# One load of v per head pair, a value factor per pair, and the rescaling of kT moved from ScalarE to VectorE, in a clustered-attention and feed-forward kernel

## The chip, the cores and the metric

The kernel runs on one NeuronCore of a Trainium2 chip. The metric is the device time of one launch in microseconds, the median of several runs. A core has five engines with a queue of instructions each: TensorE (PE, matrix products), VectorE (DVE), ScalarE (ACT), GpSimd (POOL) and SyncE (SP), which here issues every DMA.

## The reference

```python
def _attn_ref(q, k, v, centroids):                 # B, H, S, D = 4, 8, 768, 64; 16 centroids per head
    q_n = q / (np.linalg.norm(q, axis=-1, keepdims=True) + 1e-06)   # k_n, c_n likewise
    q_assign = np.argmax(np.einsum('bhsd,hcd->bhsc', q_n, c_n), axis=-1)   # k_assign likewise
    mask = q_assign[:, :, :, None] == k_assign[:, :, None, :]
    scores = np.where(mask, D ** -0.5 * np.matmul(q, k.transpose(0, 1, 3, 2)), -1000000000.0)
    attn = np.exp(scores - np.max(scores, axis=-1, keepdims=True))
    attn = attn / (np.sum(attn, axis=-1, keepdims=True) + 1e-09)
    return np.matmul(attn, v)
x = attn_out.transpose(0, 2, 1, 3).reshape(3072, 512)
def _moe_ref(x, w_in, w_out):                      # 512 x 2048 and 2048 x 512
    h = x @ w_in
    g = np.where(h >= 1, h, np.where(h <= -1, 0.0, (h + 1) ** 2 / 4.0))
    return g @ w_out
```

## The kernel before

All products run on TensorE in 16-bit floats: a number is split into a high and a low half, and three of the four cross products are added. The work is cut into 4 batches; a batch has 4 pairs of heads (`hp`) and 3 chunks of 256 queries; batch and chunk together are the 12 units `u` of the feed-forward part.

For each batch and pair, `kv_load` brings k, q and v (384 KB each) into the pair's slot (`kvq`). `kv_scale` squares k and q on ACT and makes a scale per tensor from the sum (tiles `sc`, `phi`, `es`). `kq_split` and `v_split` (both through `split`) write high and low halves, ACT the high ones, DVE the low ones; `transpose` turns k and q by DMA. `assign` multiplies kT and qT with the centroids, finds the cluster of each token by five DVE steps on `mx` and `z1`, writes a one-hot row into the natural tiles `kn` and `qn` (tiles `n`, for the first batch also `x`, `g`, `o`), scales k's second half by `phi` on POOL (`n<-n,phi`) and kT by `phi` on ACT (`kvq<-kvq,phi`), writes q's high half a second time on ACT (`n<-kvq,sc`), and transposes both again (`k1`, `q1`). The scale of v is one per batch: `v_bound` takes the largest |v| of a pair on DVE (`v_am`), for batches 1 to 3 from a load of v of its own, 384 KB per pair into the tile `x` or `o`, ahead of the batch; `batch_scale` makes `sv` and `isx` from the four.

`at_scores` multiplies a query tile with all keys into PSUM (`bank`), with DVE reducing it (`sS`, `sbi`); `at_soft` takes the exponential on ACT, splits it (`hl`: ACT the cast, POOL the difference), and transposes it by DMA into `pT`, or early in the program by PE; `at_av` multiplies by the values, spreads 1/sum over PSUM, copies that on ACT (`rb<-banka`), multiplies on DVE and splits the result into `x`. `ffn1` and `ffn2` are the two products with the weights, with `r` and `g` between them: DVE, ACT, DVE, ACT cast, POOL difference.

The weights come in 16 pieces (512 KB; here each float arrives as two 32-bit words). `w_load` brings a piece to a staging place that the table `RAW` names (three places of `w`, the last two pieces in halves through `wk`); `w_bits` and `w_split` turn it into two halves with four ACT passes of 128x1024 per piece (two named `w<-w` or `wk<-w`, one `w<-w,w_sw`, one CAST), two DVE passes and two POOL passes.

The order within each engine comes from a planner in the kernel (`Recorder`, L38 to L292): every operation is recorded with a step from a table at the end of the function, and `forward` and `backward` lay them out by the prices of `price` in eight rounds. All rows of the trace therefore bear the line L292.

Of the kernel before, what the change touches and what calls it, by code (L numbers as in the profile page):

```python
# [37 lines left out]
class Recorder:  # L38
# [37 lines left out]
    def price(self, eng, op, out, ins, kw):  # L76
# [274 lines left out]
def tile_clustered_attention_moe(  # L351
# [38 lines left out]
    RAW = [0, 1, 2, 0, 1, 2, 0, 1, 0, 2, 0, 1, 0, 0, None, None]  # L390
# [20 lines left out]
    rings["vb"] = rings["o"]  # L411
# [14 lines left out]
    hid = Ring([bank_h] + halves)  # L426
    spare = Ring([x[:, 384:] for x in halves])
# [5 lines left out]
    def misc(*shape):  # L433
        return (row_banks if early() else hid)(*shape, dtype=F32)
# [26 lines left out]
    tab = const.tile([P, 1], F32, name="tab")  # L461
    rec.scalar.activation(out=tab, in_=ones[:, :1], func=AF.Sqrt)

    def centroids():
# [5 lines left out]
        nrm = const.tile([P, 1], F32, name="c_nrm")  # L470
# [3 lines left out]
        rn = const.tile([P, 1], F32, name="c_rn")  # L474
# [16 lines left out]
    def v_bound(b, hp):  # L491

        if b == 0:
            st = view(slots[hp][:, 2304:3072], [2 * T * D], F32)
        else:
            st = view(rings["x"].bufs[2], [2 * T * D], F32) if b == 1 else new("vb", [2 * T * D], F32)
            rec.sync.dma_start(st.rearrange("p (h f) -> p h f", h=2), heads(v, b, hp))
        e = BX.setdefault(b, {})
        if hp == 0:
            e["am"] = new("v_am", [NP], BF16, 2)  # L500
        rec.vector.tensor_reduce(
            out=e["am"][:, hp : hp + 1], in_=st, op=ALU.max, axis=AX.X, apply_absolute_value=True
        )

    def to_scale(iv, sc):

        tiny_and(iv, iv, EXP_MASK)
        rec.vector.tensor_scalar(out=iv, in0=iv, scalar1=TINY, scalar2=2.0**-11, op0=ALU.max, op1=ALU.mult)  # L510
        rec.vector.reciprocal(sc, iv)

    def batch_scale(b):

        e = BX[b]
        ar = misc(NP + 1)
        rec.tensor.matmul(ar[:, :NP], ones, e["am"], start=True, stop=True)
        mx = ar[:, NP:]
        isx, sv = new("isx", [1], F32, 3), new("sv", [1], F32, 3)
        rec.vector.tensor_reduce(out=mx, in_=ar[:, :NP], op=ALU.max, axis=AX.X)  # L520
        to_scale(mx, sv)
        rec.vector.tensor_copy(isx, mx)
        e.update(isx=isx, sv=sv)
# [13 lines left out]
    def kv_scale(b, hp):  # L537
        e = KV[b, hp]
        am = new("am", [2], F32, 2)
        for i, x in enumerate("kq"):  # L540
# [20 lines left out]
        rec.vector.reciprocal(sc, iv)  # L561
# [3 lines left out]
        raw, ri = ar[:, 2:3], ar[:, 3:4]  # L565
# [13 lines left out]
    def transpose(out, nat):  # L579
        rec.sync.dma_start_transpose(out=out, in_=nat.rearrange("p n a d -> p (n a d)"))  # L580

    def kq_split(b, hp):

        e = KV[b, hp]
        for x, lower, at in (("k", 0, 0), ("q", 1, 4)):
# [5 lines left out]
            transpose(e[x + "T"], nat)  # L591
# [518 lines left out]
```

## Time and profile before

| | |
|---|---|
| median of 3 runs | 921.69 us (919.97 to 922.86) |
| the profiled execution | 923.2 us, of which the trace spans 921.4 us |
| busy in the span: PE, ACT, DVE, POOL | 812.9, 691.6, 604.1, 565.6 us |
| DMA: moved, mean rate | 144.39 MB, 157 GB/s |
| HBM: read, written | 40.40 MB, 6.29 MB |

The span has a start, up to some 145 us, in which weights and the first batch are prepared and PE is idle for more than half of the time, and a long remainder in which PE is busy nearly throughout. A row of a window table shows which of the two a stretch is. The rows come from the one profiled execution, the median from runs without a profile.

### The profile page before, as it was taken

The page shows a single profiled execution, that of the slowest core. Times are in us where ns is not written, and L with a number is a line of the kernel's source. Part 1 is how long each engine was busy: PE and PEld are TensorE (multiplying, and loading weights), DVE is VectorE, ACT ScalarE, POOL GpSimd, SP SyncE. Part 2 cuts the span into 40 slices and gives each one's busy share as a digit, 9 for nine tenths or more (in the row PEclk, how much of TensorE's full clock was granted, in tenths as well). Part 3 has the DMA queues.
Part 4 walks back from the last instruction along what each step waited for, and adds up shares of the span by engine and source line. Part 5 has one row for each costly group of instructions (what it writes and reads, how often), then busy time and mean ns, then how long its engine had stood idle before and what let it go on. Part 6 is the DMA issues. An engine that isn't in the chain of part 4 may idle for free.

```text
span 921.4 us, 19471 instructions
## 1 busy us (share of the span) xinstructions
PE 812.9 (88%) x7414; PEld 559.2 (61%) x7414; DVE 604.1 (66%) x1322; ACT 691.6 (75%) x1173; POOL 565.6 (61%) x520
## 2 busy tenths in 40 slices
PE   0256668988998999999989999998998999999998
PEld 0234446655766766676666666766666666666664
DVE  5998777887888565646776665547886555554222
ACT  6989997977778677778868778777887677777232
POOL 1766786975565577765555667655656677666221
PEclk9998789999999999999999999999999999999999
DMA  9979956796899958978999778888899768576100
GB/s 293 251 176 218 238 127 145 155 188 139 200 179 159 189 109 144 181 130 193 196 186 163 147 150 166 149 175 170 184 179 174 136 136 129 108 130 113 19 24 24
DMA packets 409535, 144.39 MB, mean 157 GB/s; under 512 B 386272, under 2 KB 401632, under 8 KB 409440
## 3 DMA queue, kind: packets, MB, share of 16 engines
q1 hardware_dynamic: 409440, 143.14, 77.0%
q8 instruction: 58, 0.95, 0.4%
q14 instruction: 37, 0.30, 0.1%
HBM read 40.40 MB, written 6.29 MB: 51 GB/s over the span
## 4 chain that ended last, share of the span: by engine, by line
PE 65%; DVE 10%; ACT 6%; issue 5%; POOL 3%; ACTq 0%; DVEq 0%; POOLq 0%
PE bank L292 47%; PE banka L292 10%; PE bankh L292 8%; DVE sS L292 3%; DVE r L292 2%; ACT sS L292 2%; DVE bank L292 2%; POOL hl L292 1%; ACT w L292 1%; DVE bankh L292 1%; DVE mx L292 1%; ACT hl L292 1%; POOL g L292 1%; ACT r L292 1%; DVE n L292 0%
## 5 line engine op out<-in xcount | busy, mean ns | idle before, releaser
L292 POOL TENSOR_TENSOR hl<-sS,hl 128x768 f16<-128x768 f32 x181 | 303.9, 1683 | 148.7 <-ACT hl L292 115.9
L292 PE MATMUL bank<-w,g 128*128 128x512 f16 x1152 | 271.1, 379 | 0.3 <-POOL g L292 0.2
L292 PEld LDWEIGHTS <-w 128*128 128x128 f16 x2304 | 224.4, 98 | 66.8 <-issue 23.0
L292 DVE CUSTOM_DVE_ANT_0 sS<-bank,zero,er 128x768 f32<-128x768 f32 x192 | 194.3, 1012 | 97.7 <-PE bank L292 67.8
L292 PEld LDWEIGHTS <-kvq 128*64 128x64 f16 (+1 forms) x3264 | 191.1, 106 | 86.2 <-issue 41.3
L292 ACT ACTIVATE sS<-sS,sbi 128x768 f32<-128x768 f32 x192 | 179.2, 933 | 83.9 <-DVE sbi L292 80.2
L292 POOL TENSOR_TENSOR g<-r,g 128x512 f16<-128x512 f32 x96 | 112.6, 1173 | 122.8 <-ACT g L292 119.2
L292 PEld LDWEIGHTS <-g 128*128 128x128 f16 x1152 | 110.7, 98 | 119.1 <-issue 2.1
L292 PE MATMUL bank<-kvq 128*128 128x384 f16 x768 | 162.4, 336 | 19.3 <-DVE sbi L292 14.1
L292 ACT CAST hl<-sS 128x768 f16<-128x768 f32 x181 | 148.3, 825 | 4.9 <-DMA pT<-hl 3.7
L292 PE MATMUL bank<-x,w 128*128 128x256 f16 x1032 | 123.9, 272 | 10.5 <-DVE r L292 5.2
L292 ACT ACTIVATE r<-r,f_ra,f_rs 128x512 f32<-128x512 f32 x96 | 77.8, 810 | 70.7 <-DVE r L292 69.7
L292 PE MATMUL banka<-pT,kvq 128*64 128x256 f16 x1728 | 106.4, 279 | 0.0
L292 DVE TENSOR_SCALAR r<-bank,f_lo,f_hi 128x512 f32<-128x512 f32 x64 | 51.6, 807 | 51.0 <-PE bank L292 41.9
L292 POOL TENSOR_TENSOR w<-w 128x1024 f32<-128x1024 f32 (+1 forms) x28 | 59.8, 2143 | 33.9 <-ACT w L292 32.0
L292 ACT CAST g<-r 128x512 f16<-128x512 f32 x96 | 58.8, 612 | 25.2 <-DVE r L292 18.7
L292 DVE SCALAR_TENSOR_TENSOR r<-bank,f_gs,r 128x512 f32<-128x512 f32 x64 | 47.9, 749 | 24.3 <-ACT r L292 15.6
L292 PE MATMUL bank<-wk,w 128*128 128x256 f16 x504 | 61.1, 272 | 3.1 <-DVE bank L292 2.1
L292 PE MATMUL bankh<-x,w 128*128 128x256 f16 x504 | 60.1, 273 | 2.2 <-DVE r L292 2.0
L292 PEld LDWEIGHTS <-ones 128*128 128x128 bf16 x244 | 17.2, 107 | 53.5 <-issue 38.5
L292 DVE TENSOR_SCALAR r<-bankh,f_lo,f_hi 128x512 f32<-128x512 f32 x32 | 25.8, 806 | 25.4 <-PE bankh L292 19.8
L292 ACT ACTIVATE n<-kvq,sc 128x768 f16<-128x768 f32 x42 | 37.1, 924 | 1.7 <-DVE sc L292 1.6
(158 smaller groups left out, 842.5 us busy)
## 6 DMA issues: line engine op xcount, KB each, us to landing
w<-in_moe_w_in_dram SPq DMA_DIRECT2D x14, 512.0 KB, 4.8
w<-in_moe_w_out_dram SPq DMA_DIRECT2D x14, 512.0 KB, 4.7
kvq<-in_k_dram SPq DMA_DIRECT2D x16, 384.0 KB, 3.6
kvq<-in_q_dram SPq DMA_DIRECT2D x16, 384.0 KB, 3.8
kvq<-in_v_dram SPq DMA_DIRECT2D x16, 384.0 KB, 4.1
out_dram<-o SPq DMA_DIRECT2D x11, 512.0 KB, 3.0
o<-in_v_dram SPq DMA_DIRECT2D x8, 384.0 KB, 3.7
pT<-hl SPq DMA_TRANSPOSE x181, 4.0
```

The lines of the kernel that those rows point to most:

```text
L292: fn(*args, **kw)
```

## The change

- `v_bound` is gone, with its own loads of v (12 of 384 KB). `kv_scale` takes the pair's |v| maximum from the slot, on DVE, and makes a value scale per pair (third column of `sc`) with three small DVE steps; `v_split` uses it. `batch_scale` forms the batch's common scale `isx` and a factor per pair, `conv`, which ACT multiplies in when it copies 1/sum (`rb<-banka,conv`).
- In `assign`, kT is scaled by `phi` on DVE instead of ACT. The halves of k and q change places, so that q's high half needs no second writing, and POOL's scaling of k stands ahead of the one-hot.
- The four transposes of the very first pair are made by PE, with eight copies from PSUM, four on ACT and four on DVE.
- Weights are staged in eight places; 15 pieces come whole, one in halves. In the last unit `r` is taken from the three buffers of `hl` instead of one.
- The planner's price of TensorE work changes, and with it the whole order.

```diff
-            if op == "transpose":
-                n *= 2
-            elif ins[1].dtype == F32:
+            if ins[1].dtype == F32:
                 n *= 4
-            return n / 4.8 + 1.2 if half else max(n / 2.4 + 2.5, 24)
+
+            return n / 4.8 + 9 if half else max(n / 2.4 + 2.5, 24)
...
-    RAW = [0, 1, 2, 0, 1, 2, 0, 1, 0, 2, 0, 1, 0, 0, None, None]
+    RAW = [3, 4, 5, 6, 7, 4, 5, 6, 0, 7, 6, 7, 0, 7, 0, None]
...
-    rings["vb"] = rings["o"]
...
-    def v_bound(b, hp):
...
-            st = view(rings["x"].bufs[2], [2 * T * D], F32) if b == 1 else new("vb", [2 * T * D], F32)
-            rec.sync.dma_start(st.rearrange("p (h f) -> p h f", h=2), heads(v, b, hp))
...
+        isx, sv, conv = new("isx", [1], F32, 3), new("sv", [1], F32), new("conv", [NP], F32, 2)
+        rec.vector.tensor_reduce(out=isx, in_=e["iv"], op=ALU.max, axis=AX.X)
+        rec.vector.reciprocal(sv, isx)
+        rec.vector.tensor_scalar(out=conv, in0=e["iv"], scalar1=sv, scalar2=None, op0=ALU.mult)
...
+        rec.vector.tensor_reduce(
+            out=am[:, 2:], in_=e["v"].rearrange("p j f -> p (j f)"), op=ALU.max, axis=AX.X, apply_absolute_value=True
+        )
...
+        tiny_and(mv, mv, EXP_MASK)
+        rec.vector.tensor_scalar(out=iv, in0=mv, scalar1=TINY, scalar2=2.0**-11, op0=ALU.max, op1=ALU.mult)
+        rec.vector.reciprocal(sc[:, 2:], iv)
...
-    def transpose(out, nat):
-        rec.sync.dma_start_transpose(out=out, in_=nat.rearrange("p n a d -> p (n a d)"))
+    def transpose(b, hp, out, nat):
+        nat = nat.rearrange("p n a d -> p (n a d)")
+        if b or hp >= 1:
+            rec.sync.dma_start_transpose(out=out, in_=nat)
+            return
...
+                    rec.tensor.transpose(ps[:, x, i * P : (i + 1) * P], nat[:, (x * T + i) * P : (x * T + i + 1) * P], idb)
+            eng = (rec.scalar.copy, rec.vector.tensor_copy)[x]
+            eng(out[:, x], ps[:, x, : T * P])
...
-        for x, lower, at in (("k", 0, 0), ("q", 1, 4)):
+        for x, lower, at in (("k", 1, 0), ("q", 0, 4)):
...
-        split(vs[:, 0], vs[:, 1], e["v"], BX[b]["sv"])
+        split(vs[:, 0], vs[:, 1], e["v"], e["sc"][:, 2:])
...
+            out=kn[:, :, 1], in0=kn[:, :, 0], in1=e["phi"].unsqueeze(2).to_broadcast([P, n2, D]), op=ALU.mult
...
-        rec.scalar.activation(out=kf, in_=kf, func=AF.Copy, scale=e["phi"])
-        qf = e["q"].rearrange("p j (t d) -> p (j t) d", d=D)
-        rec.scalar.activation(out=qn[:, :, 1], in_=qf, func=AF.Copy, scale=e["sc"][:, 1:2])
...
+        rec.vector.tensor_scalar(out=kf, in0=kf, scalar1=e["phi"], scalar2=None, op0=ALU.mult)
...
-        rec.scalar.copy(rs, rb)
+        rec.scalar.activation(out=rs, in_=rb, func=AF.Copy, scale=BX[b]["conv"][:, hp : hp + 1])
...
-        r = new("r", [2 * CQ], F32, 1)
+
+        r = new("hl" if u == NU - 1 else "r", [2 * CQ], F32, 1)
...
-            at((b - 1) * SB + 22 + hp * 3 if b else PRO + 1, v_bound, b, hp)
-        at(b * SB - 13 if b else -7, batch_scale, b)
+        at(b * SB + LA - 0.6, batch_scale, b)
...
-        t0 = PRO + 2 + i if last is None else wat[last] + 0.1
+        t0 = max(PRO + 2 + i, -1 if not RAW[i] else PRO) if last is None else wat[last] + 0.1
```

What the order of the engines becomes, at three places. ACT in the start, where the first pair (slot `kvq_61`) has been assigned; `x_69` and `x_70` are the natural tiles of the third pair, `w_76` or `w_73` the weights. Before:

```order
L292 ACTIVATE x_70,am_135<-kvq_63 128x768
L292 ACTIVATE w_76<-w_76,w_sw_157 128x1024
L292 ACTIVATE wk_66<-w_76 128x1024
L292 CAST w_76<-w_76 128x1024
L292 ACTIVATE n_73<-kvq_61,sc_137 128x12x64
L292 ACTIVATE kvq_61<-kvq_61,phi_141 128x1536
```

After:

```order
L291 ACTIVATE g_71,am_127<-kvq_64 128x768
L291 ACTIVATE wk_66<-w_73 128x1024
L291 ACTIVATE w_73<-w_73 128x1024
L291 COPY kvq_61<-bank_74 128x768
L291 COPY kvq_61<-bank_75 128x768
L291 ACTIVATE o_65,am_127<-kvq_64 128x768
```

The second writing of q (`n_73`) and the scaling of kT have left ACT, and two copies of PE's transposes stand there, ahead of the finished weight pieces. DVE in batch 2, between the score reductions (ISA) of batch 1 and the assignment of its first pair. Before:

```order
L292 TENSOR_SCALAR phi_141<-bankh 128x1
L292 TENSOR_SCALAR r_212<-bank_78,f_lo_187,f_hi_182 128x512
L292 SCALAR_TENSOR_TENSOR kvq_61<-kvq_61,sv_148 128x768
L292 SCALAR_TENSOR_TENSOR r_212<-bank_78,f_gs_207,r_212 128x512
L292 TENSOR_TENSOR rb_176<-banka,rb_176 128x256
L292 TENSOR_REDUCE mx_149<-bankh 128x24
```

After:

```order
L291 TENSOR_SCALAR phi_135<-bankh 128x1
L291 TENSOR_REDUCE am_127<-kvq_62 128x1
L291 TENSOR_SCALAR r_206<-bank_75,f_lo_181,f_hi_176 128x512
L291 SCALAR_TENSOR_TENSOR r_206<-bank_75,f_gs_201,r_206 128x512
L291 ISA sS_80,sbi_149<-bank_74,few,er_141 128x768
L291 ISA sbi_149 128x1
L291 SCALAR_TENSOR_TENSOR kvq_61<-kvq_61,sc_128 128x768
L291 TENSOR_SCALAR kvq_61<-kvq_61,phi_135 128x1536
L291 TENSOR_REDUCE mx_137<-bankh 128x24
```

The maximum of the next pair's v (`am_127`) and the scaling of kT now stand in DVE's row here, the latter just ahead of the assignment (`mx`) and of what follows it. DVE in the last unit, where `r_212` and `r_206` are the one buffer of `r`. Before:

```order
L292 TENSOR_SCALAR r_212<-bank_78,f_lo_189,f_hi_184 128x512
L292 SCALAR_TENSOR_TENSOR r_212<-bank_78,f_gs_209,r_212 128x512
L292 TENSOR_SCALAR r_212<-bankh,f_lo_189,f_hi_184 128x512
L292 SCALAR_TENSOR_TENSOR r_212<-bankh,f_gs_209,r_212 128x512
L292 TENSOR_SCALAR r_212<-bank_78,f_lo_189,f_hi_184 128x512
```

After:

```order
L291 TENSOR_SCALAR hl_160<-bankh,f_lo_183,f_hi_178 128x512
L291 SCALAR_TENSOR_TENSOR hl_160<-bankh,f_gs_203,hl_160 128x512
L291 TENSOR_SCALAR hl_158<-bank_75,f_lo_183,f_hi_178 128x512
L291 SCALAR_TENSOR_TENSOR hl_158<-bank_75,f_gs_203,hl_158 128x512
L291 TENSOR_SCALAR hl_159<-bank_75,f_lo_183,f_hi_178 128x512
L291 SCALAR_TENSOR_TENSOR hl_159<-bank_75,f_gs_203,hl_159 128x512
```

The order is the same, the tile is another one of three each time.

## Rows read from the trace of the kernel before

**Rows 1.** Window table: stretch and length in us, then busy us of each engine.
```profile
core 0: us, PE busy (x) PEld busy (x) DVE busy (x) ACT busy (x) POOL busy (x), PEclk, DMA share, GB/s
0.00:20.00 20.00, 1.18 (x9) 1.06 (x10) 9.68 (x27) 12.00 (x19) 3.84 (x26) 1.00 0.91 285
20.00:60.00 40.00, 13.50 (x167) 10.34 (x167) 38.41 (x82) 33.90 (x39) 26.85 (x16) 1.00 0.94 244
60.00:145.00 85.00, 55.22 (x518) 38.10 (x518) 67.51 (x167) 79.85 (x119) 60.84 (x51) 0.82 0.80 182
145.00:200.00 55.00, 48.35 (x437) 33.36 (x434) 46.66 (x122) 48.81 (x94) 44.76 (x38) 1.00 0.82 165
200.00:300.00 100.00, 93.45 (x899) 63.98 (x898) 83.00 (x187) 77.15 (x132) 57.50 (x53) 1.00 0.85 170
...
440.00:520.00 80.00, 74.32 (x739) 51.54 (x738) 57.25 (x127) 61.95 (x107) 46.60 (x44) 0.98 0.94 176
...
640.00:720.00 80.00, 74.81 (x717) 50.60 (x716) 60.16 (x132) 63.77 (x107) 47.45 (x43) 1.00 0.94 181
720.00:880.00 160.00, 160.00 (x1389) 110.61 (x1387) 76.22 (x151) 105.78 (x191) 96.68 (x91) 1.00 0.59 106
```

**Rows 2.** Timeline, start of one in us, its length, engine, what: start and tail.
```profile
14.04 8.96 SPq L292 DMA_TRANSPOSE kvq<-n  x2
...
23.71 0.81 PE L292 MATMUL bank<-cT,kvq 128*128 128x16 f16 x24 [0.50 <-DVE w_sw L292]
...
47.33 1.48 PE L292 MATMUL bank<-kvq 128*128 128x384 f16 x4
...
56.56 0.93 ACT L292 ACTIVATE sS<-sS,sbi 128x768 f32<-128x768 f32 x1 [2.85 <-DVE sbi L292]
...
67.03 1.54 PE L292 MATMUL bank<-idf,sS 128*128 128x128 f32 x6 [3.35 <-ACT sS L292]
...
145.42 0.81 ACT L292 ACTIVATE r<-r,f_ra,f_rs 128x512 f32<-128x512 f32 x1
...
882.07 1.47 PE L292 MATMUL bank<-x,w 128*128 128x256 f16 x12 [1.31 <-DVE r L292]
...
897.47 1.47 PE L292 MATMUL bank<-x,w 128*128 128x256 f16 x12 [0.91 <-DVE r L292]
```

**Rows 3.** Groups of ACT up to 145 us: form and count, busy us, mean ns.
```profile
L292 ACT ACTIVATE w<-w,w_sw 128x1024 f32<-128x1024 f32 x13 | 16.0, 1227 | 3.2 <-POOL w L292 2.0 <-DVE w_sw L292 1.2
L292 ACT ACTIVATE w<-w 128x1024 f32<-128x1024 f32 x13 | 14.8, 1138 | 0.0
L292 ACT ACTIVATE wk<-w 128x1024 f32<-128x1024 f32 x13 | 14.7, 1133 | 3.4 <-DMA w<-in_moe_w_out_dram 2.8 <-DVE bank L292 0.5
L292 ACT CAST w<-w 128x1024 f16<-128x1024 f32 x13 | 14.6, 1125 | 0.1
L292 ACT CAST pT<-bank 128x768 f16<-128x768 f32 x11 | 8.7, 791 | 0.1
L292 ACT ACTIVATE kvq<-kvq,phi 128x1536 f16<-128x1536 f16 x4 | 6.3, 1570 | 0.0
L292 ACT ACTIVATE n<-kvq,sc 128x768 f16<-128x768 f32 x6 | 5.4, 924 | 0.0
```

**Rows 4.** Groups of DVE over the whole span, same columns.
```profile
L292 DVE TENSOR_SCALAR wk<-wk 128x1024 uint32<-128x1024 uint32 x14 | 13.1, 938 | 3.0 <-ACT wk L292 2.7
L292 DVE TENSOR_TENSOR pT<-bank,pT 128x768 f16<-128x768 f32 x11 | 10.5, 951 | 1.8 <-ACT pT L292 1.8
L292 DVE TENSOR_REDUCE v_am<-o 128x1 bf16<-128x768 f32 x8 | 7.5, 943 | 0.0
L292 DVE RECIPROCAL sc<-bank 128x2 f32<-128x2 f32 x11 | 1.8, 164 | 0.2
```

**Rows 5.** Timeline near 50 us: DVE beside POOL, and the same DVE form at 19.93.
```profile
19.93 0.69 DVE L292 TENSOR_SCALAR wk<-wk 128x1024 uint32<-128x1024 uint32 x1 [1.91 <-ACT wk L292]
...
48.46 2.43 DVE L292 SCALAR_TENSOR_TENSOR x<-kvq,sc,x 128x768 f16<-128x768 f32 x1
...
50.61 2.04 POOL L292 TENSOR_TENSOR w<-w 128x1024 f32<-128x1024 f32 x1 [0.53 <-ACT w L292]
...
51.28 1.91 DVE L292 TENSOR_SCALAR wk<-wk 128x1024 uint32<-128x1024 uint32 x1
```

**Rows 6.** The loads of v of their own: DMA issues, and SP's waits behind them.
```profile
o<-in_v_dram SPq DMA_DIRECT2D x8, 384.0 KB, 3.7
...
SPq L292 <- DVE v_am L292: 13.3, 6, 5.0
```

**Rows 7.** What PE waited for from 440 to 520 us: total us, times, longest.
```profile
PE bank L292 <- DVE sbi L292: 2.7, 3, 1.5
PE bank L292 <- DVE r L292: 0.8, 2, 0.6
```

More of the change, by code (lines that the diff above doesn't have):

```diff
@@ L417, in tile_clustered_attention_moe @@
     rings["g"] = Ring([gb[:, :512], gb[:, 512:]])
-    nats = [tiles(f"n{i}", 2, 3072) for i in range(2)] + [rings["x"].bufs[1:3], [gb] + rings["o"].bufs]
+    nb = tiles("n", 1, 4 * 3072)[0]
+    nats = [[nb[:, (2 * i + x) * 768 : (2 * i + x + 1) * 768] for x in range(2)] for i in range(2)]
+    nats += [rings["x"].bufs[1:3], [gb] + rings["o"].bufs]
     wb = tiles("w", 1, 2 * NF * 4096)[0]
-    raws = [wb[:, (2 * NF - n) * 1024 : (2 * NF - n + 2) * 1024] for n in (2, 4, 6)]
+    raws = [wb[:, n * 2048 : (n + 1) * 2048] for n in range(NF)]
+    raws[0] = nb[:, :2048]
+    ends = [wk[1], nb[:, 2048:]]
     bank = [psum.tile([P, 1024], F32, name=f"bank{i}") for i in range(3)]
@@ L426, in tile_clustered_attention_moe @@
     hid = Ring([bank_h] + halves)
+    start = iter([0, 1] * 2).__next__
     spare = Ring([x[:, 384:] for x in halves])
@@ L489, in heads @@
         return src[b, 2 * hp : 2 * (hp + 1)].rearrange("h (p t) d -> p h (t d)", t=T)
-    def v_bound(b, hp):
-        if b == 0:
-            st = view(slots[hp][:, 2304:3072], [2 * T * D], F32)
-        else:
-            st = view(rings["x"].bufs[2], [2 * T * D], F32) if b == 1 else new("vb", [2 * T * D], F32)
-            rec.sync.dma_start(st.rearrange("p (h f) -> p h f", h=2), heads(v, b, hp))
[L498 to L511, printed above, removed]
     def batch_scale(b):
         e = BX[b]
[L516 to L523, printed above, removed]
+        isx, sv, conv = new("isx", [1], F32, 3), new("sv", [1], F32), new("conv", [NP], F32, 2)
+        rec.vector.tensor_reduce(out=isx, in_=e["iv"], op=ALU.max, axis=AX.X)
+        rec.vector.reciprocal(sv, isx)
+        rec.vector.tensor_scalar(out=conv, in0=e["iv"], scalar1=sv, scalar2=None, op0=ALU.mult)
+        e.update(isx=isx, conv=conv)
     def kv_load(b, hp):
@@ L538, in kv_scale @@
         e = KV[b, hp]
-        am = new("am", [2], F32, 2)
+        am = new("am", [3], F32, 2)
         for i, x in enumerate("kq"):
@@ L545, in kv_scale @@
             )
-        ar = misc(4)
+        rec.vector.tensor_reduce(
+            out=am[:, 2:], in_=e["v"].rearrange("p j f -> p (j f)"), op=ALU.max, axis=AX.X, apply_absolute_value=True
+        )
+        ar = misc(5)
         ah = am.bitcast(BF16).rearrange("p (n a) -> p n a", a=2)[:, :, 1]
-        rec.tensor.matmul(ar[:, :2], ones, ah, start=True, stop=True)
-        sc = new("sc", [2], F32, 2)
+        rec.tensor.matmul(ar[:, :3], ones, ah, start=True, stop=True)
+        sc = new("sc", [3], F32, 2)
         iv = ar[:, :2]
@@ L560, in kv_scale @@
         )
[L561 removed]
+        rec.vector.reciprocal(sc[:, :2], iv)
+        if hp == 0:
+            BX[b] = dict(iv=new("v_iv", [NP], F32, 3))
+        mv, iv = ar[:, 2:3], BX[b]["iv"][:, hp : hp + 1]
+        tiny_and(mv, mv, EXP_MASK)
+        rec.vector.tensor_scalar(out=iv, in0=mv, scalar1=TINY, scalar2=2.0**-11, op0=ALU.max, op1=ALU.mult)
+        rec.vector.reciprocal(sc[:, 2:], iv)
         es, ph = new("es", [1], F32, 2), new("phi", [1], F32, 2)
[L565 removed]
+        raw, ri = ar[:, 3:4], ar[:, 4:5]
         rec.vector.tensor_scalar(
@@ L577, in split @@
         rec.vector.scalar_tensor_tensor(out=lo, in0=src, scalar=sc, in1=hi, op0=ALU.mult, op1=ALU.subtract)
-    def transpose(out, nat):
-        rec.sync.dma_start_transpose(out=out, in_=nat.rearrange("p n a d -> p (n a d)"))
+    def transpose(b, hp, out, nat):
[3 more added lines that the diff above has]
+            return
+        ps = view(bank[start() if hp == 0 else 2], [2, 4 * 256], BF16)
+        nat, out = nat.bitcast(BF16), out.bitcast(BF16).rearrange("p (x n) q -> p x (n q)", x=2)
+        for x in range(2):
+            with rec.group():
+                for i in range(T):
+                    rec.tensor.transpose(ps[:, x, i * P : (i + 1) * P], nat[:, (x * T + i) * P : (x * T + i + 1) * P], idb)
+            eng = (rec.scalar.copy, rec.vector.tensor_copy)[x]
+            eng(out[:, x], ps[:, x, : T * P])
     def kq_split(b, hp):
         e = KV[b, hp]
-        for x, lower, at in (("k", 0, 0), ("q", 1, 4)):
+        for x, lower, at in (("k", 1, 0), ("q", 0, 4)):
             nat = e[x + "n"]
@@ L856, in w_load @@
         n = RAW[2 * f + a]
-        st = wk[1][:, : 512 * wd] if n is None else raws[n][:, : 1024 * wd]
+        st = ends[part][:, : 512 * wd] if n is None else raws[n][:, : 1024 * wd]
         if a == 0:
```

28 lines of the change are left out of this document (14 added, 14 removed).

## The prediction

> **What bounds the kernel now.** I read the window table first [rows 1]. Two stretches have to be told apart. Up to 145 us PE is busy for 1.18 + 13.50 + 55.22 = 69.9 us, less than half, while ACT is busy for 12.00 + 33.90 + 79.85 = 125.75 us, so it has 19.25 us idle, 8 of them in the first 20 us while the loads come in. DVE has its peak from 20 to 60 us, with 38.41 of 40 us, and 115.6 of 145 us in all. So the start is paced by ACT with DVE close behind, PE waits. From 145 us, where ACT handles the first hidden activation [rows 2], PE takes over: it is idle for 6.65 us up to 200 us, for 6.55, 5.68 and 5.19 us in the three stretches in which the next batch's pairs are prepared (200 to 300, 440 to 520, 640 to 720 us), and not at all from 720 to 880 us. PE does the same products after the change, so the time can only come from PE's idle time: about 75 us in the start, 24 us in the stretches named, and what the tail holds.
>
> **What the change removes from the start.** I count what stands in ACT's row ahead of the first hidden activation, before and after: 22 exponentials, 11 casts `hl`, 11 casts `pT` and 4 casts `x` in both, so the attention is equally far. Gone are the four scalings of kT, 6.3 us, and four second writings of q (12 writings become 8), 4 x 0.924 = 3.7 us [rows 3]. Added are four copies of PE's transposes from PSUM; the nearest row is the cast of 128x768 from PSUM, 0.791 us, so 3.2 us. The scale on the copy of 1/sum is priced by the pass with a scale against the one without, 1.227 - 1.138 = 0.09 us [rows 3], so 0.4 us for the four here and 4.3 us for all 48; past the start ACT has room for these. That is 10.0 - 3.6 = 6.4 us less for ACT.
>
> Also fewer weight passes stand ahead of that point: 13 of each of four before, and 13, 12, 12 and 11 after, 1.14 + 1.23 + 2 x 1.12 = 4.6 us [rows 3]. They are put off, not saved. ACT has 6.2 us idle from 145 to 200 us, and they fit there only as far as PE does not wait for those weights.
>
> The first pair no longer waits for the queue of DMAs. Its transposes were handed to SP at 14.04 us, and PE could use the first at 23.71 us; scores began at 47.33 us and the first exponential at 56.56 us [rows 2]. PE's 48 transposes of 128x128 cost at most eight times the 1.54 us that six take in 32-bit floats [rows 2], 12.3 us, and hardly under an eighth of that; both ends lie in PE's 45 idle us from 0 to 60 us [rows 1], and I take nothing for them. Without that cover they would cost their own time. In DVE's row the first score reduction has 2 weight pieces ahead of it instead of 6, and all four pairs need no common value scale for `v_split`. So attention starts some ten us earlier and weights later; this is an exchange of work between ACT and DVE, and I count no gain for it beyond the 6.4 us.
>
> **What DVE gets in exchange.** Four scalings of kT, 128x1536 in 16 bits. The trace has no such row. The nearest one is 128x1024 in 32 bits, 0.69 us alone, 0.938 us in the mean and 1.91 us beside POOL [rows 4, 5]. The lower end is half the clean row's rate, 0.5 us; the upper one the longest stall seen, 2.43 us [rows 5]. I take 1.0 us, clean rate by size, since POOL is busy in two thirds of 20 to 60 us and idle as often later. Four copies from PSUM at 0.951 us [rows 4], 3.8 us. Three small steps more per pair at 0.164 us, less those per batch, about 1.3 us. The maxima of v stay, 0.94 us each, and only change place. Together about 9 us, with 4.0 us for kT; ends 7 and 15 us.
>
> In 20 to 60 us DVE has 1.6 us free [rows 1], but there the order puts weight passes behind; from 60 to 145 us it has 17.5 us. So I take these 9 us as covered; if the cover fails, they end last, and that is the first rival. In its queue the maximum of the first v now waits for that load ahead of the centroids' scaling, which the first assignment needs; the load came third before too.
>
> The rows show how DVE and POOL meet: the same DVE pass takes 0.69 us alone and 1.91 us at 51.28 us, begun while a POOL product of 2.04 us ran [rows 5]. The Trainium skill, SBUF — State Buffer, section "SBUF: two separate sides", says why: a DVE operation that uses both port pairs and a GpSimd operation that reads SBUF lock each other out for a whole instruction. By that rule the trace agrees with the 1.91 us, and every kT scaling that meets a POOL product would cost up to that product's length; the sum above holds without it.
>
> **After the start.** At the 40th exponential in ACT's row there stand 8 finished `g` casts after the change and 5 before, and one weight piece more. So PE gets feed-forward work earlier, and part of its 6.65 idle us from 145 to 200 us can go. I take a third, 2.2 us; ends 0 and 6.65 us.
>
> The 12 loads of v are hidden anyway: 384 KB land in 3.7 us, SP's wait behind `v_am` is 13.3 us in all [rows 6], and no stretch shows PE waiting for a DMA; I take nothing. The larger number of staging places only lets weights come earlier, and ACT's wait for a weight load is 2.8 us once [rows 3]: nothing.
>
> In the three preparing stretches ACT loses 12 x (1.57 + 0.92) = 30 us, and POOL's scaling of k leaves the chain behind the one-hot. DVE gains 12 x (1.0 + 0.5) us, and the 0.94 us of the v maximum moves into them. PE's waits there end on DVE: 2.7 us on `sbi` and 0.8 us on `r` from 440 to 520 us [rows 7]. DVE is busy for 83.00 of 100, 57.25 of 80 and 60.16 of 80 us [rows 1]. One gains what the other loses, and I take nothing; ends are a third of the 17.4 idle us, 5.8 us, as a gain, and the second rival's price as a loss. Queued behind the kT scaling on DVE are the assignment itself and the next `r` and `rb` steps, for which ACT waits and then PE.
>
> **The tail.** In the last unit PE waits 1.31 and 0.91 us for DVE's second pass on the only `r` buffer [rows 2]. With three buffers in turn both go: 2.2 us; what is late next is PE itself.
>
> **Sum.** 6.4 + 2.2 + 2.2 = 10.8 us. The profiled execution took 923.2 us, with 921.4 us of span; 923.2 - 10.8 = 912.4 us. The median of the runs shown is 1.5 us lower, 921.7 us, so 911 us, with its own range from 906 to 918 us.
>
> **The rivals.** First, the start is not ACT's to give: DVE's 9 us end last from 20 to 60 us, where it has 1.6 us free, or ACT's time is refilled with waiting, as its 19 idle us show that it waits already. Then the ACT relief and the pick-up bring nothing and only the tail's 2.2 us are left: 919.5 us. For it speaks the saturated window, against it that ACT idles only 5.2 us from 60 to 145 us. The Trainium skill, Perfetto Trace Analysis, section "Optimizing Scalar/DVE Operations", says that with a saturated DVE it may make sense to move work to ScalarE; the change does the reverse in just that window, and by that rule this case would be right.
>
> Second, slower: in the preparing stretches of batches 1 to 3 DVE's new work stands in the row ahead of score reductions and `r` steps, for which PE waits. The price is 1.0 + 0.5 + 0.94 = 2.4 us per pair, 29 us for 12 pairs if all of it ends last, half of that if the rest lies beside PE work. It decides from 10.8 / 12 = 0.9 us per pair. With half, 911 + 14.5 = 925.5 us, with all 940 us. For it speaks [rows 7]; against it that DVE is free for 17 to 28% of these stretches.
>
> Third, more: PE is filled from the first hidden activation on, all 6.65 us go, and with ACT relieved also a third of the 17.4 us: 6.4 + 6.65 + 2.2 + 5.8 = 21 us, 901 us.
>
> **How the numbers follow.** Forecast 0.50; first rival 0.20; second 0.13; third 0.17. A measurement of this kernel tells about 0.3% from no change, that is 918.9 to 924.5 us. Faster: 0.50 + 0.17 + 0.05 of the first rival = 0.72; same: the rest of it, 0.15; slower: 0.13. The range from 901 to 925 us leaves out half of the third rival and most of the second, 0.17 together.
>
> **What would show it.** Right: first exponential before 50 us, first hidden activation near 139 us, ACT busy for 16 x 2.49 - 3.2 - 4.3 = 32 us less in all, no kT scaling on ACT, PE without the two gaps in the tail. The first rival: DVE without idle time from 20 to 60 us and the first hidden activation still near 145 us. The second: PE idle for more than 17 us in the three preparing stretches, ended by DVE. The third: PE idle for under 1 us between first hidden activation and the 200 us mark. The forecast is wrong if kT scalings on DVE take over 2 us each, or if the new order of TensorE's work opens gaps in the stretch without any now.

## The result, and the profile after

The changed kernel takes 923.4 us in the median (920.5 to 925.1, 20 runs), the kernel before 920.8 us (919.0 to 924.5, 20 runs) on the same chip. The ratio is 1.0022, with an interval from 1.0013 to 1.0032. That is slower by 2.6 us by the medians and by 2.0 us by the ratio: the interval leaves out 1, but the difference is inside the 0.3% that the prediction counted as no change. I had forecast 911 us, a gain of 10.8 us. The profiled execution, with 925.1 us the longest of the 20, spans 923.3 us.

The window table after, to be read beside [rows 1] (columns as there):

```profile
0.00:20.00 20.00, 4.39 (x74) 4.14 (x74) 11.15 (x32) 12.60 (x22) 4.68 (x27) 1.00 0.89 298
20.00:60.00 40.00, 20.96 (x202) 14.09 (x202) 39.24 (x100) 32.01 (x46) 19.69 (x15) 0.55 0.93 243
60.00:145.00 85.00, 55.97 (x492) 40.76 (x494) 69.20 (x155) 71.51 (x104) 60.02 (x47) 0.71 0.66 152
145.00:200.00 55.00, 49.83 (x444) 33.70 (x441) 46.42 (x132) 51.01 (x93) 52.08 (x38) 1.00 0.69 141
200.00:300.00 100.00, 90.87 (x871) 61.31 (x869) 83.93 (x187) 73.59 (x131) 63.12 (x55) 1.00 0.87 174
300.00:440.00 140.00, 136.11 (x1249) 95.00 (x1248) 82.83 (x171) 101.21 (x184) 94.44 (x86) 0.99 0.77 144
440.00:520.00 80.00, 75.19 (x746) 51.99 (x746) 66.70 (x147) 56.60 (x99) 46.10 (x43) 1.00 0.98 176
...
640.00:720.00 80.00, 75.14 (x714) 49.81 (x715) 65.48 (x149) 54.74 (x96) 50.79 (x45) 0.96 0.97 176
720.00:880.00 160.00, 159.07 (x1381) 109.81 (x1379) 77.14 (x153) 107.42 (x194) 95.20 (x90) 1.00 0.60 110
```

In the first 145 us ACT is busy for 12.60 + 32.01 + 71.51 = 116.1 us instead of 125.75 us. Some 4.5 us of this are weight passes put off, the rest is the relief. So the relief came; but the first hidden activation hardly moved (below), and ACT's idle time grew by as much, from 19.25 to 28.9 us. In the views of what ACT waited for up to 145 us, the waits for DVE add up to 13.5 us (9.2 before) and those for PE to 6.1 us (none before). The largest of each (us in total, times, longest):

```profile
ACT wk L291 <- DVE w L291: 5.6, 3, 2.8
...
ACT kvq L291 <- PE bank L291: 3.2, 3, 2.4
```

The second line is ACT waiting for PE's transposes, to copy them. DVE has 0.76 us free from 20 to 60 us. PE is idle for 9.1 us from 200 to 300 us (6.55 before) and for 3.9 us from 300 to 440 us, where the same window of the kernel before is this row:

```profile
300.00:440.00 140.00, 138.69 (x1272) 96.20 (x1270) 84.90 (x175) 105.54 (x191) 93.33 (x85) 1.00 0.84 158
```

PE was idle there for 1.3 us, so these two stretches hold 5.2 us more idle time than before. Idle time is not the whole of it: the granted clock after is 0.99 from 300 to 440 us and 0.96 from 640 to 720 us, where it was 1.00 before (which in turn had 0.98 from 440 to 520 us), and products at the lower of the two levels take longer and count as busy (twelve of them 2.66 instead of 1.47 us near 310 us, in the rows on kT's scalings below). The timeline of ACT after answers [rows 2] (start in us, length, engine, what):

```profile
39.49 0.94 ACT L291 ACTIVATE sS<-sS,sbi 128x768 f32<-128x768 f32 x1
...
144.88 0.83 ACT L291 ACTIVATE r<-r,f_ra,f_rs 128x512 f32<-128x512 f32 x1
```

The first exponential comes 17 us earlier (56.56 before), the first hidden activation 0.5 us earlier (145.42). The groups of DVE up to 145 us (form and count, busy us, mean ns) show what it got:

```profile
L291 DVE TENSOR_SCALAR kvq<-kvq,phi 128x1536 f16<-128x1536 f16 x4 | 6.4, 1602 | 0.0
...
L291 DVE TENSOR_REDUCE am<-kvq 128x1 f32<-128x768 f32 x4 | 3.8, 942 | 0.6 <-DMA kvq<-in_v_dram 0.6
L291 DVE COPY kvq<-bank 128x768 bf16<-128x768 bf16 x4 | 2.1, 548 | 0.0
```

The chain of work that ended last, as shares of the span by engine, first before and then after, shows DVE's share grown from 10 to 16%:

```profile
PE 65%; DVE 10%; ACT 6%; issue 5%; POOL 3%; ACTq 0%; DVEq 0%; POOLq 0%
```

```profile
PE 66%; DVE 16%; POOL 5%; issue 5%; ACT 5%; DMA 2%; SPq 1%; ACTq 0%; DVEq 0%; POOLq 0%
```

And in the tail PE runs without the two gaps of [rows 2]:

```profile
886.02 1.48 PE L291 MATMUL bank<-x,w 128*128 128x256 f16 x12
887.33 2.75 PE L291 MATMUL bank<-w,g 128*128 128x512 f16 x12
890.03 2.78 PE L291 MATMUL bank<-x,w 128*128 128x256 f16 x24
```

### The profile page after: what moved, and what is told of

Read it like the earlier page. It is cut to its first block, busy times and chain, and to the rows that moved or that the text cites. A ratio compares the mean times of both kernels' runs of the same rounds, so it can differ in the third digit from the quotient of the medians.

```text
span 923.3 us, 19539 instructions
## 1 busy us (share of the span) xinstructions
PE 824.1 (89%) x7458; PEld 566.8 (61%) x7458; DVE 621.0 (67%) x1375; ACT 664.3 (72%) x1145; POOL 573.4 (62%) x521
## 4 chain that ended last, share of the span: by engine, by line
PE 66%; DVE 16%; POOL 5%; issue 5%; ACT 5%; DMA 2%; SPq 1%; ACTq 0%; DVEq 0%; POOLq 0%
PE bank L291 49%; PE banka L291 9%; PE bankh L291 8%; DVE sS L291 3%; DVE r L291 2%; POOL hl L291 2%; DVE bank L291 2%; DVE n L291 2%; POOL g L291 1%; ACT w L291 1%; DVE kvq L291 1%; ACT sS L291 1%; DVE w L291 1%; DVE wk L291 1%; POOL n L291 1%
## 5 line engine op out<-in xcount | busy, mean ns | idle before, releaser
L291 POOL TENSOR_TENSOR hl<-sS,hl 128x768 f16<-128x768 f32 x181 | 308.0, 1707 | 133.7 <-ACT hl L291 124.7
L291 DVE CUSTOM_DVE_ANT_0 sS<-bank,few,er 128x768 f32<-128x768 f32 x192 | 194.2, 1012 | 96.0 <-PE bank L291 74.9
L291 PEld LDWEIGHTS <-kvq 128*128 128x128 f16 (+1 forms) x3264 | 191.5, 107 | 83.7 <-issue 35.5
L291 POOL TENSOR_TENSOR g<-r,g 128x512 f16<-128x512 f32 x88 | 105.8, 1202 | 90.8 <-ACT g L291 90.5
L291 ACT ACTIVATE r<-r,f_ra,f_rs 128x512 f32<-128x512 f32 x88 | 71.4, 812 | 56.8 <-DVE r L291 56.4
L291 DVE TENSOR_SCALAR r<-bank,f_lo,f_hi 128x512 f32<-128x512 f32 x59 | 47.7, 808 | 46.8 <-PE bank L291 38.9
L291 ACT CAST g<-r 128x512 f16<-128x512 f32 x88 | 53.7, 610 | 14.9 <-DVE r L291 8.6
L291 POOL TENSOR_TENSOR w<-w 128x1024 f32<-128x1024 f32 (+1 forms) x24 | 49.1, 2051 | 24.0 <-ACT w L291 23.7
L291 DVE SCALAR_TENSOR_TENSOR n<-kvq,sc,n 128x768 f16<-128x768 f32 x28 | 41.0, 1484 | 0.6 <-ACT n L291 0.4
L291 POOL TENSOR_TENSOR n<-n,phi 128x768 f16<-128x768 f16 x14 | 25.1, 1791 | 23.0 <-PE bank L291 12.9
```

The costliest lines, as they stand in the source:

```text
L291: fn(*args, **kw)
```

## The experiments

An edit of this kernel makes the planner lay out the order of all engines anew (only the edit of the tail, below, left it as it was up to the last unit). So there are two kinds of run: **planned**, where the order is new, and **kept**, where the operation is recorded and priced as ever, but issued to another engine or not at all, so that each engine's row stays as it was. Each ratio is against the kernel before on the same chip, whose median was 920.6 to 921.7 us.

### Is it the engine of the kT scaling?

First, the changed kernel with the kT scalings issued to ACT, order kept:

```
-rec.vector.tensor_scalar(out=kf, in0=kf, scalar1=e["phi"], ...)
+rec.add("vector", "tensor_scalar", <issues nc.scalar.activation(kf, Copy, scale=phi)>, ...)
```

> The changed kernel with the 16 scalings of kT issued to ScalarE instead of VectorE, every engine's order otherwise kept row by row (the planner still sees them as VectorE work). Theory 1, VectorE: the scalings, 1.03 us each in the mean and 1.60 us in the start, end last in 20 to 100 us and in 230 to 320 us; without them the lead of some 7 us that TensorE had at 230 us is kept, and the kernel takes 915 to 919 us against 923.4. Theory 2, the new order costs the time, not the engine: 922 to 925 us, as the order is the same. Theory 3, ScalarE is as late as VectorE at these places: 925 us or more, with its 1.57 us per scaling ahead of exponentials.

Measured: 927.1 us, ratio 1.0068 (1.0046 to 1.0090), 3.7 us slower than with DVE, as theory 3 had it. (In this run and the next the small tile `sv` also lies in another place.) DVE had time from 20 to 60 us, and it did not help:

```profile
20.00:60.00 40.00, 19.75 (x202) 13.81 (x202) 34.68 (x94) 32.98 (x44) 19.18 (x15) 0.74 0.90 239
```

DVE is busy for 34.68 instead of 39.24 us here, yet PE gets through the same 202 products in this stretch as in the changed kernel. Theory 1 is out in this form: with ACT in DVE's place nothing is won. What DVE's scalings cost by themselves is priced further down. The same edit, planned:

```
-rec.vector.tensor_scalar(out=kf, in0=kf, scalar1=e["phi"], ...)
+rec.scalar.activation(out=kf, in_=kf, func=AF.Copy, scale=e["phi"])
```

> The changed kernel with the scalings of kT on ScalarE and planned as such, so that the whole order is laid out anew. Theory 1: 914 to 919 us, at least as good as with the order kept. Theory 2 (the order decides): anything between 917 and 930 us, with no relation to the run with the order kept. Theory 3: 925 us or more.

Measured: 932.7 us, ratio 1.0129 (1.0103 to 1.0155). The instructions are those of the run above; the order alone makes 5.6 us. The reverse, on the kernel before, order kept:

```
-rec.scalar.activation(out=kf, in_=kf, func=AF.Copy, scale=e["phi"])
+rec.add("scalar", "activation", <issues nc.vector.tensor_scalar(kf, phi, mult)>, ...)
```

> The kernel before with the 16 scalings of kT issued to VectorE, every engine's order otherwise kept. Theory 1: VectorE pays 4 x 1.6 us in a start in which it has 1.6 us free from 20 to 60 us, and 12 x 0.8 us in the preparing stretches, of which a third to a half shows: 925 to 930 us against 920.8. Theory 2: 920 to 922 us. My forecast's reasoning, ScalarE being relieved of 6.3 us in the start: 915 us.

Measured: 929.9 us, ratio 1.0092 (1.0068 to 1.0115). So in either order the scaling is dearer on the engine for which the order was not made: 3.7 us on ACT in the new order, 8.7 us on DVE in the old one.

### The tail alone

```
-r = new("r", [2 * CQ], F32, 1)
+r = new("hl" if u == NU - 1 else "r", [2 * CQ], F32, 1)
```

> The kernel before with r in the last unit taken from the three hl buffers, nothing else changed up to the last unit. If the tail's two gaps of 1.31 and 0.91 us are worth their length: 918.5 us against 920.8. If something else ends the program: 920.8 us.

Measured: 918.2 us, ratio 0.9972 (0.9958 to 0.9985), a gain of 2.6 us. The order differs only in the last unit, where PE's timeline has no gap left:

```profile
879.26 1.47 PE L292 MATMUL bank<-x,w 128*128 128x256 f16 x12
880.57 2.75 PE L292 MATMUL bank<-w,g 128*128 128x512 f16 x12
883.16 2.78 PE L292 MATMUL bankh<-x,w 128*128 128x256 f16 x24
```

This version beats both kernels. If the tail is worth as much in the changed kernel, where its two gaps are gone as well, the rest of the change costs 923.4 - 918.2 = 5.2 us.

### The price of PE's work, which sets the order

The new price in the kernel before, the old one in the changed kernel, and a price of 10 in place of 9:

```
-return n / 4.8 + 1.2 if half else max(n / 2.4 + 2.5, 24)     # and without: if op == "transpose": n *= 2
+return n / 4.8 + 9 if half else max(n / 2.4 + 2.5, 24)
```

> The kernel before with only the planner's new price of TensorE work (no doubled transpose, 9 instead of 1.2 ns on the short products), so the same instructions in a newly laid out order. The engine of the kT scalings did not explain the missing gain, so now theory 2, the order: if the new price is what the change needs, 915 to 919 us against 920.9; if the order costs the gain, 924 to 932 us, since this order was not made for ScalarE's kT scalings. If an order laid out anew makes little of a difference: 919.5 to 922.5 us.

Measured: 926.3 us, ratio 1.0062 (1.0044 to 1.0079).

> The changed kernel with the planner's old price of TensorE work. Theory 2, the order costs the gain: 913 to 920 us against 923.4. If the new price was needed: 926 us or more. If the price is without effect: 922 to 925 us.

Measured: 924.7 us, ratio 1.0044 (1.0027 to 1.0060), so the order with the old price is not where the gain lies.

> The changed kernel with 10 instead of 9 ns in the planner's price of a short product, a change without meaning of its own that lays the order out anew. It tells how far one order lies from the next: within 922 to 925 us if orders are all alike; 3 us or more off, up or down, if each order is a draw with a spread as large as what the change does.

Measured: 923.1 us, ratio 1.0028 (1.0012 to 1.0044). The changed kernel's three orders lie within 1.6 us of each other. Those of the kernel before do not, as the price in its own line shows when it goes from 1.2 to 1.3 and to 1.0, with the very same instructions:

```
-return n / 4.8 + 1.2 if half else ...
+return n / 4.8 + 1.3 if half else ...
```

> The kernel before with 1.3 instead of 1.2 ns in the planner's price of a short product, nothing else: the same instructions in an order laid out anew. If orders are all alike: 920 to 922 us. If the order of before is one of the better draws, which would explain why every part alone made it slower: 925 to 935 us.

Measured: 925.8 us, ratio 1.0053 (1.0039 to 1.0066).

> The kernel before with 1.0 instead of 1.2 ns in the planner's price of a short product: the same instructions in a third order. If the order of before is a good draw out of a spread of some 5 us: 924 to 930 us. If only the order at 1.3 ns was a bad one: 919 to 922 us.

Measured: 936.7 us, ratio 1.0165 (1.0140 to 1.0190). Four orders of the kernel before thus take 920.8, 925.8, 926.3 and 936.7 us. Compared at one price, the change makes the kernel 3.9 us slower at the old price (920.8 to 924.7 us) and 2.9 us faster at the new one (926.3 to 923.4 us), so even its sign hangs on the order. Over the orders measured, the mean of the changed kernel is 923.7 us and that of the kernel before 927.4 us; three and four draws are too few to call it the better one. The first hidden activation in the two runs, 1.3 first, and one window of the second show where:

```profile
155.31 0.80 ACT L292 ACTIVATE r<-r,f_ra,f_rs 128x512 f32<-128x512 f32 x1
```

```profile
156.83 0.81 ACT L292 ACTIVATE r<-r,f_ra,f_rs 128x512 f32<-128x512 f32 x1
```

```profile
640.00:720.00 80.00, 70.64 (x713) 47.99 (x712) 59.22 (x125) 64.27 (x109) 46.08 (x43) 0.98 0.95 173
```

In both the feed-forward part begins some 10 us later, of which the first run makes good about half by the end (its median is 5.0 us above 920.8 us); in the second PE is also idle for 9.4 us from 640 to 720 us, against 5.19 us in [rows 1].

### Other parts, undone or done alone, planned

The first pair by DMA in the changed kernel:

```
-if b or hp >= 1:
+if True:
     rec.sync.dma_start_transpose(out=out, in_=nat)
```

> The changed kernel with the first pair's four transposes by DMA, as before, and no copies from PSUM. My forecast took TensorE's 48 transposes as covered by its idle time in the first 60 us and the start as paced by ScalarE: then 3.2 us of ScalarE are given back and the early scores lost, 921 to 925 us. Rival: the early scores bring nothing, because weights are put off by 13 to 25 us for them and the first hidden activation comes at the same 145 us, so that without them the kernel takes 918 to 922 us.

Measured: 925.6 us, ratio 1.0049 (1.0033 to 1.0064): PE's transposes bring some 2 us here, or the order does. The old table of weight places in the changed kernel:

```
-RAW = [3, 4, 5, 6, 7, 4, 5, 6, 0, 7, 6, 7, 0, 7, 0, None]
+RAW = [7, 6, 5, 7, 6, 5, 7, 6, 7, 5, 7, 6, 7, 7, None, None]      # the old three places
```

> The changed kernel with the old table of weight places (three places of w, the last two pieces in halves). If the eight places cost the gain: 916 to 920 us against 923.4. If they carry part of it: 926 us or more. Nothing: 922 to 925 us.

Measured: 923.8 us, ratio 1.0033 (1.0021 to 1.0044): no difference. The new table in the kernel before (the reverse edit, with its buffers):

> The kernel before with only the eight staging places for weights and their new table. If weights that come earlier take the DMA queues from the first pairs' k and q and from their transposes: 924 us or more. If they come earlier and fill ScalarE's 8 idle us of the first 20 us: 916 to 919 us. As I forecast, nothing: 920 to 922 us.

Measured: 926.3 us, ratio 1.0054 (1.0035 to 1.0073). The halves alone in the kernel before:

```
-for x, lower, at in (("k", 0, 0), ("q", 1, 4)):
+for x, lower, at in (("k", 1, 0), ("q", 0, 4)):      # and GpSimd's scaling of k ahead, as in the change
...
-rec.scalar.activation(out=qn[:, :, 1], in_=qf, func=AF.Copy, scale=e["sc"][:, 1:2])
```

> The kernel before with only the exchanged halves of k and q: no second writing of q's high half (16 writings of 0.92 us less on ScalarE), GpSimd's scaling of k ahead of the one-hot. My forecast's step, ScalarE's time in the start: 3.7 us off, 917 us. If ScalarE's time there is refilled with waiting: 920 to 922 us. If GpSimd's scaling, now in front of the assignment, meets VectorE's steps on the same natural tile: 923 to 928 us.

Measured: 933.0 us, ratio 1.0127 (1.0108 to 1.0146). The values' part alone in the kernel before, and the same with 1.3 in the price:

```
-split(vs[:, 0], vs[:, 1], e["v"], BX[b]["sv"])
+split(vs[:, 0], vs[:, 1], e["v"], e["sc"][:, 2:])      # kv_scale, batch_scale and rb as in the change
```

> The kernel before with only the values' part: v loaded once, its maximum taken from the slot with three small VectorE steps per pair, v_split with the pair's own factor, the factor brought in with the copy of 1/sum. Each undoing of another part in the changed kernel made it slower, so the loss must lie in the parts not undone yet: this one, the halves or the staging places. If this part costs it (the v maximum and its small steps now stand in VectorE's row within each pair's preparation): 925 to 932 us against 920.9. If the loads saved and the common scale's wait are a gain: 915 to 919 us. As I forecast: 920 to 922 us.

Measured: 936.1 us, ratio 1.0162 (1.0139 to 1.0184).

> The kernel before with the values' part alone, as in the earlier run, and 1.3 instead of 1.2 ns in the planner's price of a short product, so the same instructions in another order. If the 15 us were that part's own cost: 933 to 939 us. If they were mostly the order's: 922 to 930 us.

Measured: 941.6 us, ratio 1.0206 (1.0186 to 1.0226). All of these are planned, and beside four orders of one and the same kernel that lie 16 us apart they cannot price a part. The last one lies outside that span. At either price the values' part is dearer by about as much, 936.1 - 920.8 = 15.3 us and 941.6 - 925.8 = 15.8 us, so in the kernel before it may well have a cost of its own; what it costs in the changed kernel, which has it in every order that was measured, is left open.

### Parts priced with the order kept

ACT's relief alone, in the kernel before:

```
-rec.scalar.activation(out=kf, in_=kf, func=AF.Copy, scale=e["phi"])
+rec.add("scalar", "activation", <issues nothing>, ...)      # and so for the second writing of q
```

> The kernel before with ScalarE's 16 scalings of kT (and 14 to 16 second writings of q) left out, every engine's order otherwise kept; the scores are computed from kT unscaled and the second product from q's low half, so this part of the computation is missing. It prices ScalarE's relief alone: 10.0 us in the start, 30 us later. My forecast, a start paced by ScalarE: at least 6 us off, 908 to 915 us. Rival 1 of the forecast, the start is not ScalarE's to give: 918 to 921 us against 920.8.

Measured: 920.0 us, ratio 0.9991 (0.9980 to 1.0003). ACT's busy time over the span falls from 691.6 to 656.2 us, four scalings of kT and four writings of q of it ahead of the first hidden activation, and the time stays. Its windows, and what ACT waited for up to 145 us (us in total, times, longest), show why; the last two lines are those of the kernel before:

```profile
20.00:60.00 40.00, 14.22 (x167) 10.09 (x166) 38.41 (x83) 30.38 (x36) 27.62 (x17) 1.00 0.96 242
60.00:145.00 85.00, 56.35 (x558) 40.00 (x558) 70.10 (x168) 75.45 (x116) 62.50 (x51) 0.84 0.84 184
```

```profile
ACT sS L292 <- DVE sbi L292: 8.4, 9, 2.9
ACT w L292 <- POOL w L292: 3.0, 4, 0.9
...
ACT x L292 <- DVE sc L292: 2.2, 1, 2.2
```

```profile
ACT sS L292 <- DVE sbi L292: 6.5, 7, 2.8
...
ACT w L292 <- POOL w L292: 2.0, 4, 0.8
```

From 20 to 145 us ACT is busy for 7.9 us less than in [rows 1], while DVE keeps its 38.41 us of 40. ACT waits longer for DVE and POOL in place of working: up to 145 us its waits for DVE add up to 14.6 us instead of 9.2 us, those for POOL to 3.0 us instead of 2.0 us. DVE's kT scalings alone, in the changed kernel:

```
-rec.vector.tensor_scalar(out=kf, in0=kf, scalar1=e["phi"], ...)
+rec.add("vector", "tensor_scalar", <issues nothing>, ...)
```

> The changed kernel with VectorE's 16 scalings of kT left out (the scores are computed from kT unscaled, this part of the computation is missing), every engine's order otherwise kept. It prices what VectorE got: 6.4 us in the start and 10 us later. If VectorE ends last there: 915 to 919 us against 923.4, and the start's part is at least half of the gain. If these are covered, as I forecast: 921.5 to 924 us.

Measured: 920.1 us, ratio 0.9988 (0.9975 to 1.0001), so 3.3 us less than the changed kernel. The first hidden activation comes 3.4 us earlier than after (one such time is good to some 2 us: the runs with the tail alone and without the loads of v, which have the order of the kernel before up to there, had it at 143.1 and 143.3 us, it at 145.42 us; so the medians carry the verdict):

```profile
141.46 0.84 ACT L291 ACTIVATE r<-r,f_ra,f_rs 128x512 f32<-128x512 f32 x1
```

PE's larger gaps behind DVE between 200 and 320 us, on the other hand, are the same. First the changed kernel (in brackets the idle time ahead and what ended it), then without kT's scalings:

```profile
238.53 0.18 PE L291 MATMUL bank<-am,ones 128*128 128x3 bf16 x1 [1.72 <-DVE mx L291]
...
250.05 1.47 PE L291 MATMUL bank<-x,w 128*128 128x256 f16 x12 [1.47 <-DVE phi L291]
...
269.93 1.47 PE L291 MATMUL bank<-x,w 128*128 128x256 f16 x12 [1.46 <-DVE bank L291]
...
309.79 0.30 PE L291 MATMUL bankh<-n,ones 128*128 128x32 f16 x6 [1.35 <-DVE n L291]
...
310.80 2.66 PE L291 MATMUL bankh<-x,w 128*128 128x256 f16 x12 [0.72 <-DVE has L291]
```

```profile
235.13 0.18 PE L291 MATMUL bank<-am,ones 128*128 128x3 bf16 x1 [1.72 <-DVE mx L291]
...
246.43 1.47 PE L291 MATMUL bank<-x,w 128*128 128x256 f16 x12 [1.47 <-DVE phi L291]
...
266.13 1.47 PE L291 MATMUL bank<-x,w 128*128 128x256 f16 x12 [1.45 <-DVE bank L291]
...
305.67 0.30 PE L291 MATMUL bankh<-n,ones 128*128 128x32 f16 x6 [1.36 <-DVE n L291]
...
306.69 1.47 PE L291 MATMUL bankh<-x,w 128*128 128x256 f16 x12 [0.72 <-DVE has L291]
```

Five gaps, 6.72 and 6.72 us, in front of the same instructions: small products of the next pair's preparation, and feed-forward products that wait for its small steps on DVE. It is not the 0.6 to 2.2 us of a kT scaling that puts them there; whether it is the order or the other steps in DVE's row is not shown. The starts of these lines also tell where the run without the scalings is ahead: by 3.40 us at the first gap already and by 4.12 us at the fourth, so most of what the scalings cost lies in the start. (The two executions end 6.0 us apart; the twelve products behind the last gap, 2.66 against 1.47 us, make 1.2 us of it.) Last, the loads of v, in the kernel before:

```
-rec.sync.dma_start(st..., heads(v, b, hp))
+rec.add("sync", "dma_start", <issues nothing>, ...)      # the maximum reads a constant tile
```

> The kernel before with the 12 loads of v of their own left out, VectorE's maximum reading a constant tile in their place (so the value scales of batches 1 to 3 are not those of v), every engine's order otherwise kept. It prices the loads alone. As I forecast, hidden: 919.5 to 922 us. If the transfers or the waits behind them on the issuing queue cost something: 915 to 919 us.

Measured: 921.0 us, ratio 1.0002 (0.9991 to 1.0014). The loads were hidden.

## Why the prediction was wrong, step by step

**The start, 6.4 us: this step failed.** I wrote that the start is paced by ACT with DVE close behind, because ACT had 125.75 busy us of 145, and took ACT's relief as a gain of the same size. With the order kept, 10 us less of ACT in the start (and 25 us later, by the busy time) are worth 1.1 us, and by the interval between a gain of 1.8 and a loss of 0.3 us. From 20 to 145 us, 8.6 of ACT's 11.25 idle us had been waits for DVE, and its idle time grew when work was taken away. A row that pointed there was DVE's 38.41 of 40 us [rows 1]. I read the sum over the stretch instead of the window in which DVE had nothing free.

**DVE's 9 us as covered: wrong in the start, right after it.** This was the other half of the same step. The four scalings took 1.60 us each, not the 1.0 us that I chose; my ends of 0.5 and 2.43 us held them. The reason for that choice misread [rows 1]: POOL is not idle for two thirds of the time later, it is busy for 60.84 of 85 us from 60 to 145 us. The copies from PSUM took 0.55 us each instead of 0.95 us. With the small steps that is still some 10 us, and leaving only the kT scalings out gave back 3.3 us. In the three preparing stretches the scalings are covered but for about 1 us: PE is idle there for 18.8 us with them and for 17.8 us without. Both signs of my first rival came: DVE with next to no idle time from 20 to 60 us, the first hidden activation still near 145 us. Of it I had said that only the tail's 2.2 us are left, 919.5 us, and gave it 0.20. That is closer than my forecast, and still 4 us low.

The Trainium skill, Perfetto Trace Analysis, section "Optimizing Scalar/DVE Operations", says that with a saturated DVE it may make sense to offload work to ScalarE. In the kernel before the trace agrees: the reverse cost 8.7 us there. In the changed kernel, whose DVE is fuller still, giving the scalings back to ACT cost 3.7 us, so here the measurement does not bear the advice out. One reading is that in the new order the scaling lies on the path from the assignment to the first scores, where ACT's 1.57 us stand ahead of exponentials; the two runs show the prices, not that reading.

**The earlier attention as an exchange without a gain: right in its result.** First exponential 17 us earlier, first hidden activation 0.5 us earlier. With DMA transposes instead the time was 925.6 us, but planned anew, which is too coarse to price it. A term that I had not counted is the 3.2 us that ACT waited for PE's transposes.

**The pick-up from 145 to 200 us, 2.2 us: came and was lost.** PE's idle time there fell from 6.65 to 5.17 us. But the two stretches up to 440 us then hold 5.2 us more idle time than before. I took nothing for the new order. With a price that changes by a tenth of a nanosecond, the same instructions moved by 5 us, and with another one by 16 us, more than any part that could be priced. That is the term missing in my sum, and it has no sign one could read from the trace before: the order of the kernel before is the best of the four that were measured, so in these draws whatever displaced it lost. My last sign of being wrong came too, if weakly: from 720 to 880 us, where PE had no idle time, it now has 0.93 us, nearly all at 730 us in a wait for DVE's `r`.

**My second rival** had the sign that PE is idle for more than 17 us in the three preparing stretches. It is 9.13 + 4.81 + 4.86 = 18.8 us, but the sign was badly set, since the kernel before has 17.4 us there already. Nor is its mechanism shown: the work of kT on DVE does not make the gaps between 200 and 320 us. Whether the moved maximum of v does was not tried with the order kept. That 923.4 us lies between 901 and 925 us is therefore luck: the upper end stood there for this rival.

**The tail, 2.2 us: right**, 2.6 us measured alone. **The v loads and the staging places, nothing: right** for the loads (921.0 us) and, planned, for the places in the changed kernel (923.8 us). **ACT busy 32 us less:** it is 27.3 us (691.6 to 664.3).

**How it adds up.** Priced with the order kept: tail -2.6, ACT's relief -1.1, DVE's kT scalings +3.3 us, together -0.4 us. The change measured +2.6 us. The remaining 3.0 us are the new order with all that could not be priced apart from it: PE's transposes, the halves, the moved maximum of v and its small steps, and what PE lost at the lower clock. They lie well inside the spread of orders; which of them it is stays open, since each replans, and the 3.3 and 1.1 us were taken in different orders, so the sum is no more than a rough one.

## What to carry to other kernels

Two engines that are both nearly full are not relieved by moving work between them: look for the window in which one has no idle time at all, take an idle engine's waits there as a sign of who paces, and prove it by leaving the work out with the order kept. Where a planner lays out the order, price each part with the order kept, by issuing the same slot to another engine or not at all, and measure two or three orders of the same instructions before a difference of 1% is put down to a part. Ship the parts whose order stays: the three buffers of the tail alone gave 918.2 us, better than the whole change.

## What the runs showed of the hardware

The same kT scaling has two prices. In the timeline of the changed kernel, DVE and then POOL:

```profile
249.92 0.60 DVE L291 TENSOR_SCALAR kvq<-kvq,phi 128x1536 f16<-128x1536 f16 x1
...
276.89 1.68 DVE L291 TENSOR_SCALAR kvq<-kvq,phi 128x1536 f16<-128x1536 f16 x1
```

```profile
276.69 1.46 POOL L291 TENSOR_TENSOR n<-n,phi 128x768 f16<-128x768 f16 x1
```

The first met no GpSimd work (its last product had ended at 247.97 us, the next began at 251.86 us). The second began 0.20 us into a product that ended at 278.15 us, and ended itself 0.42 us after that. The Trainium skill, SBUF — State Buffer, section "SBUF: two separate sides", has whichever comes first hold the shared ports for its whole instruction; the trace agrees with that: the scaling took 1.1 us more than alone.

The 1.00 in the first two rows of [rows 1] is no reading of the clock. The window table gives 1.00, the level of 2.4 GHz, for 0 to 60 us, but the trace's clock records begin only at 63.5 us, and in PE's timeline the same eight products take 1.01 us before and 0.62 us later:

```profile
25.75 1.01 PE L292 MATMUL bank<-wk,ones 128*128 128x128 bf16 x8 [1.23 <-DVE wk L292]
...
138.38 0.62 PE L292 MATMUL bank<-wk,ones 128*128 128x128 bf16 x8 [1.23 <-DVE sbi L292]
```

In the changed kernel, whose table gives 0.55 for 20 to 60 us, they take as long:

```profile
36.74 1.01 PE L291 MATMUL bank<-wk,ones 128*128 128x128 bf16 x8
```

So the 1.00 of before and the 0.55 of after in 20 to 60 us do not show a difference of speed. And the gaps of 1.35 and 0.72 us near 310 us were followed by twelve products in 2.66 us in the changed kernel and in 1.47 us in the run without kT's scalings: after equal gaps PE went on at a lower clock in one execution and not in the other (granted clock 0.91 and 1.00 from 300 to 320 us).
